# Groups of three, two and three gate units at fixed places, with W' parts, exponentials, h copies and w_in pairs moved

## The chip, the core and the metric

The kernel runs on one core of a Trainium2 chip. The metric is device time in microseconds (us), lower is better: the median of three runs. The engines are named as the profile names them: PE (TensorE matmuls), PEld (its weight loads), DVE (VectorE), ACT (ScalarE), POOL (GpSimd) and SP (SyncE, which issues transfers).

## What is computed

```python
def sm_attn(qq, kk, vv):                     # scale = 1/8
    s = scale * np.matmul(qq, kk.transpose(0, 1, 3, 2))
    s = s - np.max(s, axis=-1, keepdims=True)
    a = np.exp(s)
    a = a / (np.sum(a, axis=-1, keepdims=True) + 1e-09)
    return np.matmul(a, vv)
p_packed = sm_attn(p, k, v)                  # p: (8, 8, 32, 64); q, k, v: (8, 8, 576, 64)
out = sm_attn(q, p_packed, p_packed)
x = out.transpose(0, 2, 1, 3).reshape(4608, 512)
h = x @ w_in                                 # (512, 2048)
sp = np.maximum(h, 0.0) + np.log1p(np.exp(-np.abs(h)))
g = h * erf(sp)
result = g @ w_out                           # (2048, 512)
```

So an attention through 32 packed rows feeds a feed-forward layer whose gate is h times erf of softplus of h.

## The kernel before, in words

The second attention and `w_in` are merged: for each batch b and each quarter j of the 2048 columns, PE multiplies the packed values by `w_in` to W'(b, j), and h is W' times the second attention's weights. Each product is kept precise by splitting its operands in a high and a low half, so W' is copied out of PSUM twice: a high part (`wph`, line 594) and a low part (`wpl`, line 601), together "the W' parts".

The feed-forward work is cut into 128 units. A unit is 256 columns of h for half of a batch's tokens (288 columns), and from unit 32 on unit 32 + 16(b - 2) + 8c + i is the i-th of half c of batch b; h, t, hs, gh and gl of that unit are named b_c_i. The units run one after another. In step n:

- PE computes the two halves of h of unit n (12 matmuls, line 623) and then the output of unit n - 5 in four quarters d (24 matmuls, line 676);
- ACT copies the two halves of h out of PSUM into hs (line 633) and computes softplus (line 639);
- when n is in `ENDS`, a group of units is closed: ACT computes erf of every unit in it (line 642) and DVE multiplies it with h (the gate, line 646). One group means one load of ACT's softplus table and one of its erf table;
- DVE splits the gated value of unit n - 3 into gh (line 652) and gl (line 659).

h goes through two PSUM banks, so the first half of the h of unit n + 1 can start only when ACT has copied the first half of unit n. The output of a unit is copied with a scale (`put`: `ob`, lines 689 and 691) and sent off when its eighth unit is done.

The attention of a later batch is cut into pieces (`yield`), and tables of pairs (unit, place) say where each piece stands in the steps; so do tables for the W' products and their parts. Place 5 is behind the h copies, 0 and 1 behind the first output quarter, 3 behind the third, and 2 at the end of the step, behind the erfs and gates. One piece holds the two exponentials of the first attention (`a`, line 473, which need DVE's maximum `m`, line 448), and the next has PE's transposes of the result (`t`, line 423). The second attention has its exponential on line 317 (`ta`). An exponential needs another ACT table. From batch 4 on W' is multiplied from `w_in` in 16-bit pairs (`wi16`, lines 254 and 259), made by DVE in eight pieces. Instructions stand on each engine in the order in which the code is run.

Of the kernel before, what the change touches and what calls it, by code (L numbers as in the profile page):

```python
# [15 lines left out]
ALU = mybir.AluOpType  # L16
# [29 lines left out]
def tile_pack_attention_moe(ctx: ExitStack, tc: tile.TileContext, qT, kT, v, pT, w_in, w_out, outT):  # L46
    nc = tc.nc
    P = 128
    B, _, NC, S = qT.shape
    DFF = w_in.shape[1]  # L50
    DM = w_out.shape[1]
    HT = S // 2
# [13 lines left out]
    NB0 = 2  # L66
# [2 lines left out]
    ALONE = 2 * HB  # L69
    TAGS = ("hs", "hs", "hs", "t1", "t1", "t1", "hs", "hs")  # L70
    BANKS = {3: 0, 4: 2}
    ENDS = tuple(range(1, 16 * B, 3))
    BEGUN = 20

    cpool = ctx.enter_context(tc.tile_pool(name="const", bufs=1))
# [83 lines left out]
    rho, omega, gate_scales = {}, {}, {}  # L159
# [102 lines left out]
    def is_narrow(b, j):  # L262

        return b >= NB0 + 2
# [3 lines left out]
    def in_turn(ins):  # L268

        if functions:  # L270
# [9 lines left out]
    ATTEND = {  # L280
# [6 lines left out]
    SCORES = ((-12, 2), (-6, 0), (-6, 1), (-4, 0), (-4, 1))  # L287
    POOLED = ((-2, 3), (-2, 2), (-1, 3), (-1, 2), (0, 0), (0, 1))
    PACKED = ((1, 0), (1, 1), (2, 0), (2, 1), (4, 0), (4, 1))
    ATTEND_LATER = (  # L290
        SCORES + ((-4, 2), (-1, 5), (-1, 3), (-1, 2), (0, 0), (0, 1), (0, 3), (0, 2)) + PACKED
        + ((5, 2), (6, 2), (8, 5), (8, 3), (8, 2), (8, 2), (9, 2), (10, 2), (10, 2)),
        SCORES + ((-4, 2), (-2, 5)) + POOLED + PACKED
        + ((5, 2), (6, 2), (7, 5), (7, 2), (8, 2), (8, 2), (9, 2), (10, 2), (10, 2)),
        SCORES + ((-4, 2), (-3, 5)) + POOLED + PACKED
        + ((5, 2), (6, 2), (9, 5), (9, 3), (9, 2), (9, 2), (10, 2), (11, 2), (11, 2)))
    BESIDE = ((1, 1), (1, 3), (B - 1, 1), (B - 1, 3))
    JOINS = {2: (25, 27, 30, 32)}
    JOINS_LATER, PAIRED = (-6, -4, 2, 4), (-4, -4, 1, 1)
# [279 lines left out]
    def w_prime_parts(b, j):  # L579
        f0, n = PIECES[j]  # L580
        at = b, f0 // FB
        if at not in wp:
            wp[at] = [wpool.tile([P, 2, FB], F32R if b < NB0 else F16, name=f"wp{x}{b}_{j}", tag=f"wp{x}") for x in "hl"]
        parts = [w[:, :, f0 % FB:f0 % FB + n] for w in wp[at]]
        if len(raw[b, j]) == 3:
            return [parts + [raw[b, j][2][:, :, 0:n]]]
        return [[w[:, r, :] for w in parts] + [raw[b, j][r][:, 0:n]] for r in range(2)]

    def w_prime_high(b, j, copy=nc.scalar.copy):
        for hi, lo, ps in w_prime_parts(b, j):  # L590
            if b < NB0:
                copy(hi, ps)
            else:
                nc.vector.tensor_scalar(hi, ps, 2.0 ** -15 if is_narrow(b, j) else rho[b][:], None, op0=ALU.mult)  # L594

# [10 lines left out]
    def h_half(n, k):  # L606
        b, c, i = units[n][:3]
        if k == 0:
            turn = sum(n > e for e in ENDS) % 2
            tag = TAGS[n] if n < ALONE else "t1" if turn else "hs"  # L610
            rows[n] = tpool.tile([P, 2, HT], F32, name=f"hs{b}_{c}_{i}", tag=tag)
        f = (2 * i + k) * P
        j, fo = f // FB, f % FB
        whi, wlo = wp[b, j]
        if n in BANKS:
            ps = ps_o.tile([P, 512], F32, name=f"h{b}_{c}_{i}_{k}", tag=f"ps_o{BANKS[n] + k}")
        else:
            ps = ps_h.tile([P, 512], F32, name=f"h{b}_{c}_{i}_{k}", tag="ps_h")
        m = 0
        ahi, alo = a2[b]  # L620
        for r in range(2):
            for w, a in ((whi, ahi), (whi, alo), (wlo, ahi)):
                nc.tensor.matmul(ps[:, 0:HT], w[:, r, fo:fo + P], a[:, r, c * HT:(c + 1) * HT],  # L623
                                 start=(m == 0), stop=(m == 5))
                m += 1
        banks_of[n, k] = ps

    def h_copy(n, k, copy=nc.scalar.copy):
        dst, src = rows[n][:, k, :], banks_of.pop((n, k))[:, 0:HT]
        if n < GROUPED:  # L630
            copy(dst, src)  # L631
        else:
            nc.scalar.mul(dst, src, 2.0 ** -18)  # L633

    def softplus(n):
        b, c, i = units[n][:3]
        ts[n] = tpool.tile([P, 2, HT], F32, name=f"t{b}_{c}_{i}", tag="t0")
        scale = 1.0 if n < GROUPED else gate_scales[b][:, 0:1]
        in_turn(nc.scalar.activation(ts[n][:], rows[n][:], AF.Softplus, scale=scale))  # L639
# [22 lines left out]
    acc = {}  # L662
    begun = set()

    def o_part(n, d):

        b, c, i, first, last = units[n]
        g = gs[n]
        w_hi, w_lo = (wo_hi, wo_lo) if b < NB0 else (half_hi, half_lo)
        if first:  # L670
            acc[b, c, d] = ps_o.tile([P, 512], F32, name=f"o{b}_{c}_{i}_{d}", tag=f"ps_o{d}")
        for k in range(2):
            f = 2 * i + k
            terms = [(wo, g[0])] if len(g) == 1 else [(w_hi, g[0]), (w_hi, g[1]), (w_lo, g[0])]
            for m, (w, gg) in enumerate(terms):
                nc.tensor.matmul(acc[b, c, d][:, 0:HT], w[f][:, d * P:(d + 1) * P], gg[:, k, :],  # L676
                                 start=(first and k == 0 and m == 0),
                                 stop=(last and k == 1 and m == len(terms) - 1))

    def put(n, d, fast=False):  # L680

        b, c, i = units[n][:3]
        t0 = b * S + c * HT
        ob = tpool.tile([P, HT], F32, name=f"ob{b}_{c}_{i}_{d}", tag="ob", bufs=NDM)
        if b < NB0:
            nc.scalar.copy(ob[:], acc[b, c, d][:, 0:HT])  # L686
        else:
            if fast:
                nc.vector.tensor_scalar(ob[:], acc[b, c, d][:, 0:HT], omega[b][:], None, op0=ALU.mult)
            else:  # L690
                nc.scalar.mul(ob[:], acc[b, c, d][:, 0:HT], omega[b][:])
        where = outT[d * P:(d + 1) * P, t0:t0 + HT]
        if (b, c, d) in begun:
            nc.gpsimd.dma_start(where, ob[:], accum_op=ALU.add)
        else:
            (nc.gpsimd if b < NB0 else nc.sync).dma_start(where, ob[:])
        begun.add((b, c, d))


    group = []  # L700

    def split(n):
        split_high(n)
        split_low(n)

    def step(n, m):

        if n < len(units):
            for k in range(2):
                h_half(n, k)  # L710
                h_copy(n, k)
            do(n, 5)
            group.append(n)
        for d in range(NDM):
            o_part(m, d)
            if units[m][4]:
                put(m, d, n in ENDS)
            if d == 0:
                do(n, 0)
                do(n, 1)  # L720
                if n < len(units):
                    softplus(n)
            elif d == 2:
                do(n, 3)
        if m + 2 < len(units):
            split(m + 2)
        if n in ENDS:
            for part in (erf, gate):
                for x in group:
                    part(x)  # L730
            group.clear()
        do(n, 2)
# [19 lines left out]
    def slot(n, where):  # L752
        return plan.setdefault((n, where), [])

    for b in range(NB0, B):
        for j in range(NFB):
            n = JOINS[b][j] if b in JOINS else first_use[b] + (JOINS_LATER if b < B - 1 else PAIRED)[j]
            behind = 1 if (b, j) in BESIDE else 2
            for where, part in ((0, w_prime), (behind, w_prime_high), (behind, w_prime_low)):
                slot(n, where).append((part, b, j))  # L760
    for b in range(NB0, B):
        base = first_use[b - 1]
        for n, where in ATTEND.get(b) or [(base + n, where) for n, where in ATTEND_LATER[base % 3]]:
            slot(n, where).append((attend, b))

    for n, k in ((21, 5), (21, 6), (22, 7)):
# [14 lines left out]
        slot(high, 0 if i < 6 else 5).append((halve_high, i))  # L781
        slot(low, 1).append((halve_low, i))
    slot(28, 2).append((in_weights,))
    for m, n in enumerate((39, 41, 42, 44, 45, 47, 48, 50)):
        slot(n, 1).append((narrow_high, m % 4, m // 4))
        slot(n, 1).append((narrow_low, m % 4, m // 4))
    for b in range(NB0 + 1, B):
# [3 lines left out]
    def do(n, where):  # L791
        for part, *args in plan.pop((n, where), []):
            part(*args)
# [44 lines left out]
    for n in range(BEGUN, len(units) + LAG):  # L838
        step(n, n - LAG)
# [39 lines left out]
```

## Time and profile before

| | before |
|---|---|
| median of three runs | 696.69 us (696.46 to 698.27) |
| the profiled execution | 696.33 us, its span 694.5 us |
| PE busy | 674.4 us, 97% of the span |
| DVE busy | 517.1 us, 74% |
| ACT busy | 493.3 us, 71% |
| POOL busy | 53.0 us, 8% |

The span runs from the first to the last instruction of the profiled execution; 1.8 us of its time lie around it. Shares of busy time are means over a beginning (attention of two batches, weights being loaded and split) and the long run of units behind it, from about 200 us on.

### The profile page before, as it was taken

What the parts mean: (1) busy time and instruction counts of PE and PEld (TensorE: products, weight loads), DVE (VectorE), ACT (ScalarE), POOL (GpSimd) and SP (SyncE); (2) the same over time, 40 slices, a digit from 0 to 9 for tenths busy, and PEclk for the clock granted to TensorE, in tenths of its full rate; (3) what the DMA queues carried; (4) which work ended last, traced back from release to release, by engine and by line L of the source; (5) the groups of instructions that cost most, each with busy time, mean ns of one, the idle gap of its engine ahead of it and who ended that gap; (6) DMA issues with size and microseconds to landing.
All of it is one profiled execution on the core that took longest, in us unless ns stands there. A gap on an engine that the chain in (4) does not pass through costs nothing.

```text
span 694.5 us, 15657 instructions
## 1 busy us (share of the span) xinstructions
PE 674.4 (97%) x6570; PEld 537.2 (77%) x6570; DVE 517.1 (74%) x822; ACT 493.3 (71%) x814; POOL 53.0 (8%) x78
## 2 busy tenths in 40 slices
PE   8899999999999999999999999899999999999998
PEld 6587989998889776777777777667777777777776
DVE  5999998989996799786765688556684768564343
ACT  2899878966577687656685775756877667767671
POOL 2031123110442000000000000000000000000000
PEclk9999999999999999999999999999999999999999
DMA  9996556376333502230022302113021100001010
GB/s 328 399 331 213 160 179 214 106 255 179 51 63 64 138 2 94 87 98 2 19 77 86 100 1 90 43 45 99 2 90 53 35 1 10 27 1 35 1 35 35
DMA packets 34310, 66.81 MB, mean 96 GB/s; under 512 B 4032, under 2 KB 13248, under 8 KB 34240
## 3 DMA queue, kind: packets, MB, share of 16 engines
q1 hardware_dynamic: 29600, 56.31, 24.2%
q0 software_dynamic: 4352, 8.92, 4.9%
q8 instruction: 51, 0.84, 0.5%
q10 hardware_dynamic: 288, 0.59, 0.2%
q14 instruction: 19, 0.16, 0.1%
HBM read 49.81 MB, written 15.99 MB: 95 GB/s over the span
## 4 chain that ended last, share of the span: by engine, by line
PE 69%; DVE 16%; ACT 4%; DMA 4%; issue 4%; POOL 1%; SPq 0%; POOLq 0%; DVEq 0%; ACTq 0%
PE o L676 43%; PE h L623 20%; DVE hs L646 3%; PE wp L575 3%; DVE gl L659 2%; DMA wi<-w_in 2%; DMA k<-kT 2%; DVE wpl L601 1%; DVE wph L594 1%; PE p L435 1%; PE s L533 1%; DVE gh L652 1%; ACT t L642 1%; DMA scratch<-wo 1%; DVE wi L259 1%
## 5 line engine op out<-in xcount | busy, mean ns | idle before, releaser
L676 PE MATMUL o<-gh,woh 128*128 128x288 f16 x1536 | 303.3, 286 | 0.8 <-DVE gh L652 0.8
L676 PEld LDWEIGHTS <-woh 128*128 128x128 f16 x2304 | 223.6, 98 | 65.9 <-issue 10.4
L676 PE MATMUL o<-gl,woh 128*128 128x288 f16 x768 | 219.6, 286 | 0.5 <-DVE gl L659 0.5
L623 PE MATMUL h<-a2h,wph 128*128 128x288 f16 (+1 forms) x512 | 149.1, 291 | 3.1 <-ACT hs L633 1.1
L623 PE MATMUL h<-a2h,wpl 128*128 128x288 f16 (+1 forms) x512 | 147.8, 289 | 3.3 <-DVE wpl L601 2.6
L633 ACT ACTIVATE hs<-h 128x288 f32<-128x288 f32 x192 | 73.7, 405 | 106.5 <-PE h L623 106.3
L623 PE MATMUL h<-a2l,wph 128*128 128x288 f16 (+1 forms) x512 | 147.5, 288 | 0.0
L652 DVE CAST gh<-hs 128x576 f16<-128x576 f32 (+1 forms) x117 | 53.3, 455 | 113.9 <-PE o L676 113.5
L659 DVE TENSOR_TENSOR gl<-hs,gh 128x576 f16<-128x576 f32 (+1 forms) x124 | 98.1, 791 | 4.4 <-ACT gh L652 0.5
L676 PE MATMUL o<-gh,wohl 128*128 128x288 f32 x448 | 99.2, 300 | 0.9 <-ACT ob L686 0.8
L623 PEld LDWEIGHTS <-wph 128*128 128x128 f16 x768 | 74.4, 98 | 22.2 <-DVE wph L594 2.1
L646 DVE TENSOR_TENSOR hs<-t,hs 128x576 f32<-128x576 f32 x128 | 90.0, 750 | 0.7 <-ACT t L642 0.7
L676 PEld LDWEIGHTS o<-gh,wohl 128*128 128x128 f32 x448 | 74.5, 188 | 7.7 <-issue 2.7
L642 ACT ACTIVATE t<-t 128x576 f32<-128x576 f32 x128 | 78.9, 674 | 0.5
L639 ACT ACTIVATE t<-hs,gs 128x576 f32<-128x576 f32 x96 | 74.5, 776 | 2.0
L676 PE MATMUL o<-gl,wohl 128*128 128x288 f32 x224 | 66.2, 295 | 0.1
L639 ACT ACT_TABLE_LOAD x45 | 57.7, 1283 | 3.0 <-DVE hs L646 2.1
L642 ACT ACT_TABLE_LOAD x44 | 56.5, 1283 | 0.8
L623 PEld LDWEIGHTS <-wpl 128*128 128x128 f16 x384 | 37.6, 98 | 12.9 <-DVE wpl L601 3.5
L676 PEld LDWEIGHTS o<-gl,wohl 128*128 128x128 f32 x224 | 42.2, 188 | 0.3 <-DVE gl L659 0.3
L631 ACT COPY hs<-h 128x288 f32<-128x288 f32 x45 | 17.0, 397 | 15.4 <-PE h L623 15.1
L623 PEld LDWEIGHTS h<-a2h,wph 128*128 128x128 f32 x128 | 24.0, 188 | 3.9 <-issue 1.3
(129 smaller groups left out, 734.3 us busy)
## 6 DMA issues: line engine op xcount, KB each, us to landing
q<-qT SPq DMA_DIRECT2D x32, 288.0 KB, 4.3
k<-kT SPq DMA_DIRECT2D x30, 288.0 KB, 4.7
wos<-w_out SPq DMA_DIRECT2D x16, 512.0 KB, 6.2
outT<-ob SPq DMA_DIRECT2D x48, 144.0 KB, 2.2
v<-v SPq DMA_DIRECT2D x24, 256.0 KB, 4.6
wi<-w_in SPq DMA_DIRECT2D x12, 512.0 KB, 6.6
outT<-ob POOLq DMA_DIRECT2D x32, 144.0 KB, 4.0
scratch<-wo POOLq DMA_DIRECT2D x16, 256.0 KB, 3.9
```

The source lines that it names most:

```text
L259: nc.vector.scalar_tensor_tensor(narrow[c, k][:, 1], w_in_sb[:, c, 2 * k * FB:2 * (k + 1) * FB], sigma_in[:], narrow[c, k][:, 0], op0=ALU. ...
L435: nc.tensor.matmul(po[NK * c:NK * c + NK, 64 * r:64 * r + 64], a1t[0:n, r, j, NK * c:NK * c + NK], values[j][0:n, 64 * (2 * c + r):64 * (2 ...
L575: nc.tensor.matmul(ps[r][NK * c:NK * c + NK, 0:n], p[:, NK * c:NK * c + NK], w, start=(m == 0), stop=(m == len(terms) - 1), skip_group_che ...
L623: nc.tensor.matmul(ps[:, 0:HT], w[:, r, fo:fo + P], a[:, r, c * HT:(c + 1) * HT], start=(m == 0), stop=(m == 5))
L631: copy(dst, src)
L633: nc.scalar.mul(dst, src, 2.0 ** -18)
L639: in_turn(nc.scalar.activation(ts[n][:], rows[n][:], AF.Softplus, scale=scale))
L642: in_turn(nc.scalar.activation(ts[n][:], ts[n][:], AF.Erf))
L646: nc.vector.tensor_tensor(hs[:], ts.pop(n)[:], hs[:], op=ALU.mult)
L652: copy(ghi[:], gs[n][0][:])
L659: nc.vector.tensor_tensor(glo[:], hs[:], ghi[:], op=ALU.subtract)
L676: nc.tensor.matmul(acc[b, c, d][:, 0:HT], w[f][:, d * P:(d + 1) * P], gg[:, k, :], start=(first and k == 0 and m == 0), stop=(last and k = ...
```

## The change

Groups: up to unit 31 they end as before; then 33, and from 34 on every unit whose number leaves 0, 3 or 5 when divided by 8, so groups hold 3, 2 and 3 units. The outputs that DVE scaled in steps at a group's end are scaled by ACT. The high part of batch 2's W' is made by ACT. The parts of the later W' stand at place 3 (ahead of a step's erfs and gates) instead of place 2. One table places the later attentions: their exponentials stand at the end of steps that close a group. For two units in 16 the h copies are handed DVE's copy function, in place of ACT's. The eight pieces of `w_in`'s pairs stand in units 46, 47, 49, 50 and 62 to 65.

```diff
-    ENDS = tuple(range(1, 16 * B, 3))
+    ENDS = tuple(range(1, 32, 3)) + (33,) + tuple(n for n in range(34, 16 * B) if n % 8 in (0, 3, 5)) + (16 * B - 1,)
...
-    ATTEND_LATER = (
-        SCORES + ((-4, 2), (-1, 5), (-1, 3), (-1, 2), (0, 0), (0, 1), (0, 3), (0, 2)) + PACKED
...
+    ATTEND_LATER = ((-12, 2), (-6, 0), (-6, 1), (-4, 0), (-4, 1), (-4, 2), (-3, 2), (-1, 0), (-1, 1), (-1, 3), (-1, 2),
+                    (0, 0), (0, 1), (1, 0), (1, 1), (2, 0), (2, 1), (4, 0), (4, 1),
+                    (5, 2), (6, 2), (8, 2), (9, 3), (9, 2), (9, 2), (10, 2), (11, 2), (11, 2))
...
+            elif b == NB0:
+                nc.scalar.mul(hi, ps, rho[b][:])
...
+        elif copy is nc.vector.tensor_copy:
+            nc.vector.tensor_scalar(dst, src, 2.0 ** -18, None, op0=ALU.mult)
         else:
             nc.scalar.mul(dst, src, 2.0 ** -18)
...
-            if fast:
-                nc.vector.tensor_scalar(ob[:], acc[b, c, d][:, 0:HT], omega[b][:], None, op0=ALU.mult)
-            else:
-                nc.scalar.mul(ob[:], acc[b, c, d][:, 0:HT], omega[b][:])
+            nc.scalar.mul(ob[:], acc[b, c, d][:, 0:HT], omega[b][:])
...
+    AFTER = [b + n for b in range(2 * 16, 16 * B, 16) for n in (9, 14)]
...
-                h_copy(n, k)
+                h_copy(n, k, nc.vector.tensor_copy if n in AFTER else nc.scalar.copy)
...
-            behind = 1 if (b, j) in BESIDE else 2
+            behind = 1 if (b, j) in BESIDE else 2 if b == NB0 else 3
...
-    for m, n in enumerate((39, 41, 42, 44, 45, 47, 48, 50)):
+    for m, n in enumerate((46, 47, 49, 50, 62, 63, 64, 65)):
```

Three places of the order show the moves. The first is on ACT, in units 93 and 94 (5_1_5 and 5_1_6, ahead of batch 6), with the exponentials `a1_7` of the first attention of batch 7. Before, from the softplus of unit 94 on:

```order
L639 ACTIVATE t5_1_6_6937<-hs5_1_6_6914,gs5_5550 128x576
L642 ACT_TABLE_LOAD
L642 ACTIVATE t5_1_4_6811<-t5_1_4_6811 128x576
L642 ACTIVATE t5_1_5_6887<-t5_1_5_6887 128x576
L642 ACTIVATE t5_1_6_6937<-t5_1_6_6937 128x576
L633 ACTIVATE hs5_1_7_6967<-h5_1_7_0_6968 128x288
L633 ACTIVATE hs5_1_7_6967<-h5_1_7_1_6976 128x288
L473 ACT_TABLE_LOAD
L473 ACTIVATE a1_7_6643,sm7_6859<-a1_7_6643,m7_6858 128x576 x2
L639 ACT_TABLE_LOAD
```

In the changed kernel, from the softplus of unit 93 on:

```order
L636 ACTIVATE t5_1_5_6887<-hs5_1_5_6863,gs5_5547 128x576
L639 ACT_TABLE_LOAD
L639 ACTIVATE t5_1_4_6811<-t5_1_4_6811 128x576
L639 ACTIVATE t5_1_5_6887<-t5_1_5_6887 128x576
L466 ACT_TABLE_LOAD
L466 ACTIVATE a1_7_6643,sm7_6859<-a1_7_6643,m7_6858 128x576 x2
L630 ACTIVATE hs5_1_6_6920<-h5_1_6_0_6921 128x288
L630 ACTIVATE hs5_1_6_6920<-h5_1_6_1_6929 128x288
L636 ACT_TABLE_LOAD
L636 ACTIVATE t5_1_6_6943<-hs5_1_6_6920,gs5_5547 128x576
```

The exponentials have moved from behind the copies of unit 95 to ahead of the copies of unit 94. Unit 94 is one of those in `AFTER`, and its two copies stand on ACT.

The second is on DVE, at the third quarter of batch 5's W', which the h of unit 84 needs. Before, behind the split of unit 78:

```order
L540 STREAM_TRANSPOSE ta6_6129<-s2_0_6_0_6130 128x288
L540 STREAM_TRANSPOSE ta6_6129<-s2_0_6_1_6131 128x288
L652 CAST gh4_1_7_6162<-hs4_1_7_5860 128x576
L659 TENSOR_TENSOR gl4_1_7_6164<-hs4_1_7_5860,gh4_1_7_6162 128x576
L646 TENSOR_TENSOR hs5_0_0_5919<-t5_0_0_5997,hs5_0_0_5919 128x576
L646 TENSOR_TENSOR hs5_0_1_6021<-t5_0_1_6057,hs5_0_1_6021 128x576
L646 TENSOR_TENSOR hs5_0_2_6081<-t5_0_2_6142,hs5_0_2_6081 128x576
L594 TENSOR_SCALAR wph5_2_6172<-wp5_2_6104 128x1024
L601 SCALAR_TENSOR_TENSOR wpl5_2_6173<-wp5_2_6104,wph5_2_6172 128x1024
```

In the changed kernel:

```order
L533 STREAM_TRANSPOSE ta6_6131<-s2_0_6_0_6132 128x288
L533 STREAM_TRANSPOSE ta6_6131<-s2_0_6_1_6133 128x288
L589 TENSOR_SCALAR wph5_2_6158<-wp5_2_6106 128x1024
L596 SCALAR_TENSOR_TENSOR wpl5_2_6159<-wp5_2_6106,wph5_2_6158 128x1024
L649 CAST gh4_1_7_6168<-hs4_1_7_5854 128x576
L656 TENSOR_TENSOR gl4_1_7_6170<-hs4_1_7_5854,gh4_1_7_6168 128x576
```

The two parts now stand ahead of the split and of the gates.

The third is on DVE, in units 43 and 44, where h of batch 2 is split while batch 3 is prepared. Before:

```order
L594 TENSOR_SCALAR wph3_1_3525<-wp3_1_3468,rho3_3349 128x1024
L601 SCALAR_TENSOR_TENSOR wpl3_1_3526<-wp3_1_3468,rho3_3349,wph3_1_3525 128x1024
L448 TENSOR_REDUCE m4_3539<-a1_4_3333 128x2
L449 TENSOR_SCALAR m4_3539<-m4_3539 128x2
L254 TENSOR_SCALAR wi16_0_1_3568<-w_in_sb_82,sigma_in_93 128x1024
L259 SCALAR_TENSOR_TENSOR wi16_0_1_3568<-w_in_sb_82,sigma_in_93,wi16_0_1_3568 128x1024
L652 CAST gh2_1_2_3594<-hs2_1_2_3301 128x576
L659 TENSOR_TENSOR gl2_1_2_3596<-hs2_1_2_3301,gh2_1_2_3594 128x576
```

In the changed kernel:

```order
L589 TENSOR_SCALAR wph3_1_3500<-wp3_1_3459,rho3_3341 128x1024
L596 SCALAR_TENSOR_TENSOR wpl3_1_3501<-wp3_1_3459,rho3_3341,wph3_1_3500 128x1024
L649 CAST gh2_1_1_3513<-hs2_1_1_3245 128x576
L656 TENSOR_TENSOR gl2_1_1_3515<-hs2_1_1_3245,gh2_1_1_3513 128x576
L441 TENSOR_REDUCE m4_3527<-a1_4_3328 128x2
L442 TENSOR_SCALAR m4_3527<-m4_3527 128x2
L649 CAST gh2_1_2_3579<-hs2_1_2_3296 128x576
L656 TENSOR_TENSOR gl2_1_2_3581<-hs2_1_2_3296,gh2_1_2_3579 128x576
```

No piece of `w_in`'s pairs stands ahead of the split of unit 42 (2_1_2) now, and the split of unit 41 has moved behind the W' parts.

Over the whole program ACT has 113 table loads in place of 103 and still all 192 copies of h from unit 32 on; DVE has no scaling of `ob` left.

## Rows read from the trace of the kernel before

**Rows 1.** Busy time (instructions) by engine in two 20 us stretches.

```profile
core 0: us, PE busy (x) PEld busy (x) DVE busy (x) ACT busy (x) POOL busy (x), PEclk, DMA share, GB/s
...
420.00:440.00 20.00, 18.25 (x176) 13.50 (x174) 15.64 (x23) 12.06 (x22) 0.00 (x0) 1.00 0.25 79
640.00:660.00 20.00, 20.00 (x166) 15.98 (x164) 8.06 (x13) 11.79 (x20) 0.00 (x0) 1.00 0.00 1
```

**Rows 2.** PE's waits from 222 us on: total us, times, longest.

```profile
PE h L623 <- DVE wpl L601: 2.6, 3, 0.9
PE t L423 <- ACT a L473: 2.3, 6, 0.6
PE h L623 <- ACT hs L633: 1.1, 1, 1.1
PE h L623 <- DVE wph L594: 1.1, 2, 0.6
PE o L676 <- DVE gh L652: 0.8, 1, 0.8
PE o L676 <- DVE gl L659: 0.5, 1, 0.5
PE p L511 <- DVE norm L507: 0.4, 2, 0.2
```

**Rows 3.** PE's waits from 160 to 222 us.

```profile
PE row_out L192 <- DVE top_out L185: 1.2, 1, 1.2
```

**Rows 4.** Timeline of PE, units 94 and 95: start us, us, [wait and releaser].

```profile
514.45 0.29 PE L623 MATMUL h<-a2h,wph 128*128 128x288 f16 x1
...
518.86 0.29 PE L623 MATMUL h<-a2h,wph 128*128 128x288 f16 x1
...
523.31 0.55 PE L423 MATMUL t<-ident,a 128*128 128x128 f32 x3 [0.61 <-ACT a L473]
```

**Rows 5.** Timeline of DVE and PE, units 82 to 84.

```profile
458.47 0.85 DVE L540 STREAM_TRANSPOSE ta<-s 128x288 f32<-128x288 f32 x2 [2.31 <-PE s L533]
...
465.10 1.22 DVE L601 SCALAR_TENSOR_TENSOR wpl<-wp,wph 128x1024 f16<-128x1024 f32 x1
465.13 0.30 PE L623 MATMUL h<-a2h,wph 128*128 128x288 f16 x1
```

**Rows 6.** Timeline of ACT, unit 77.

```profile
435.39 0.78 ACT L473 ACTIVATE a<-a,m 128x576 f32<-128x576 f32 x1 [3.29 <-DVE m L449]
```

**Rows 7.** Timeline of DVE, unit 45.

```profile
274.17 1.28 DVE L259 SCALAR_TENSOR_TENSOR wi<-w_in_sb,sigma_in,wi 128x1024 f16<-128x1024 f32 x1
```

**Rows 8.** Timeline of DVE, unit 26.

```profile
165.31 1.28 DVE L594 TENSOR_SCALAR wph<-wp,rho 128x1024 f16<-128x1024 f32 x1
```

**Rows 9.** Timeline of ACT, units 93 to 95.

```profile
512.70 0.78 ACT L639 ACTIVATE t<-hs,gs 128x576 f32<-128x576 f32 x1
515.38 0.41 ACT L633 ACTIVATE hs<-h 128x288 f32<-128x288 f32 x1 [1.91 <-PE h L623]
...
517.35 1.28 ACT L642 ACT_TABLE_LOAD   x1
518.65 1.83 ACT L642 ACTIVATE t<-t 128x576 f32<-128x576 f32 x3
...
521.09 1.28 ACT L473 ACT_TABLE_LOAD   x1
522.39 0.77 ACT L473 ACTIVATE a<-a,m 128x576 f32<-128x576 f32 x1
...
524.03 1.28 ACT L639 ACT_TABLE_LOAD   x1
```

**Rows 10.** ACT's groups from 222 us on: busy us, mean ns | idle before.

```profile
L642 ACT ACT_TABLE_LOAD x31 | 39.8, 1283 | 0.5
...
L691 ACT ACTIVATE ob<-o,omega 128x288 f32<-128x288 f32 x32 | 15.0, 497 | 16.7 <-PE o L676 16.7
...
L317 ACT ACTIVATE ta<-ta 128x1152 f32<-128x1152 f32 x5 | 5.8, 1164 | 1.3 <-DVE ta L315 1.2
```

**Rows 11.** Busy time by engine from 222 us on, columns as in rows 1.

```profile
222.00:694.50 472.50, 460.26 (x4520) 352.19 (x4519) 319.81 (x503) 321.81 (x521) 2.90 (x4) 1.00 0.16 50
```

More of the change, by code (lines that the diff above doesn't have):

```diff
@@ L283, in tile_pack_attention_moe @@
             (29, 1), (29, 2)),
[1 row of a table removed]
[1 row of a table added]
             (36, 0), (36, 1), (37, 0), (37, 1), (38, 0), (38, 0), (38, 0), (38, 1),
[1 row of a table removed]
-    SCORES = ((-12, 2), (-6, 0), (-6, 1), (-4, 0), (-4, 1))
-    POOLED = ((-2, 3), (-2, 2), (-1, 3), (-1, 2), (0, 0), (0, 1))
-    PACKED = ((1, 0), (1, 1), (2, 0), (2, 1), (4, 0), (4, 1))
-    ATTEND_LATER = (
-        SCORES + ((-4, 2), (-1, 5), (-1, 3), (-1, 2), (0, 0), (0, 1), (0, 3), (0, 2)) + PACKED
[L292 to L296, printed above, removed]
[1 row of a table added]
+    ATTEND_LATER = ((-12, 2), (-6, 0), (-6, 1), (-4, 0), (-4, 1), (-4, 2), (-3, 2), (-1, 0), (-1, 1), (-1, 3), (-1, 2),
+                    (0, 0), (0, 1), (1, 0), (1, 1), (2, 0), (2, 1), (4, 0), (4, 1),
+                    (5, 2), (6, 2), (8, 2), (9, 3), (9, 2), (9, 2), (10, 2), (11, 2), (11, 2))
     BESIDE = ((1, 1), (1, 3), (B - 1, 1), (B - 1, 3))
@@ L678, in o_part, with put @@
                                  stop=(last and k == 1 and m == len(terms) - 1))
-    def put(n, d, fast=False):
+    def put(n, d):
         b, c, i = units[n][:3]
@@ L716, in step @@
             if units[m][4]:
-                put(m, d, n in ENDS)
+                put(m, d)
             if d == 0:
@@ L762, in tile_pack_attention_moe @@
         base = first_use[b - 1]
-        for n, where in ATTEND.get(b) or [(base + n, where) for n, where in ATTEND_LATER[base % 3]]:
+        for n, where in ATTEND.get(b) or [(base + n, where) for n, where in ATTEND_LATER]:
             slot(n, where).append((attend, b))
```

4 rows, old and new, of the table ATTEND are left out of this document.

## The prediction

> **What bounds the kernel now.** I read four views in this order. The first is busy time in 20 us stretches. Where no attention runs, PE is busy for all of its 20.00 us, its granted clock is 1.00, that is 2.4 GHz, and 165 to 166 matmuls fit, one each 0.12 us; at 420 us it is busy for 18.25 us at the same clock [rows 1]. So PE sets the pace everywhere, DVE and ACT have spare time (319.8 and 321.8 of 472.5 us busy from 222 us on, 68% each [rows 11]), and nothing can be won but what PE waits.
>
> The second view, PE's own waits, says how much that is. From 222 us on there are 16 waits, 8.8 us together [rows 2]. A wait costs more than its row: a matmul's row lasts 0.29 us [rows 4], while in a full stream the next one starts after 0.12 us, so a stop loses the wait and about 0.16 us of overlap. 8.8 + 16 x 0.16 = 11.4 us is all that the stretch holds. Ahead of it one more wait matters, 1.2 us, in which PE waits for DVE's tallest weight, `top_out` [rows 3].
>
> The third view, the timelines, says why PE waits. There are three causes. (a) The W' parts stand behind three gates on DVE: `wpl` runs from 465.10, and the h that needs it has already begun at 465.13 [rows 5]. That is 2.6 + 1.1 us in five waits. (b) The exponentials of the first attention stand directly ahead of PE's transposes: PE waits 0.61 us at 523.31 [rows 4], in six waits 2.3 us [rows 2]. Once it is worse: ACT itself waits 3.29 us for DVE's maximum with the copies of h queued behind the exponential [rows 6], and the 1.1 us wait of h for hs is that. (c) DVE is late in the forties because pieces of `w_in`'s pairs stand ahead of the splits [rows 7]: 0.8 + 0.5 us. Two small waits for `norm`, 0.4 us, come from the one of the three old tables that places the normalisation behind a unit's last outputs.
>
> **The change, part by part.** *W' parts.* In unit 82 the transposes `ta` start on DVE at 458.47 and take 0.85 us [rows 5]. The two parts, 1.22 us each, now follow at once, so they end near 461.8; the h of unit 84 starts at 465.13. They have 3.3 us to spare, and what they push back, one split and the gates, is needed more than a unit later, at 4.41 us a unit (518.86 - 514.45 [rows 4]). Batches 3 and 6 are the same with the last quarter. Gain: 3.7 + 5 x 0.16 = 4.5 us.
>
> *Exponentials two units earlier.* They now end two units ahead of the transposes instead of directly ahead, so PE's six waits go: 2.3 + 6 x 0.16 = 3.3 us. The maximum `m` now never stands behind a group's gates, since unit base - 4 closes no group, so the 3.29 us stop on ACT goes and with it 1.1 + 0.16 = 1.3 us. But the exponentials now stand ahead of copies of h, and this I work out from the units where before has everything but the move. Softplus of unit 93 starts at 512.70 [rows 9]. Then come: softplus 0.78, a table load 1.30 (517.35 to 518.65), two erfs 1.22 (two thirds of 1.83), a table load 1.30, two exponentials 1.64 (522.39 to 524.03), the first copy of unit 94 0.41. That ends at 519.35. The h of unit 95 would start at 518.86 [rows 4]. So PE waits 0.5 us, in each of four batches: a cost of 2.0 us. Behind the next softplus ACT is on time again: it has no more than a copy, a load and a softplus to do in that unit.
>
> *The copies on DVE don't take place.* The order shows the copies of unit 94 on ACT. `copy is nc.vector.tensor_copy` compares two method objects that are made anew at each access, which is never true, so the branch for DVE is dead. Were it alive, those 2.0 us would be hidden; I count them in full.
>
> *The other exponential,* `ta`, now stands behind a group's three erfs and ahead of copies. With unit 94's times: the erfs end at 518.65 + 1.83 = 520.48; load 1.30, exponential 1.16 [rows 10], copy 0.41 end at 523.35, 8.90 us behind the unit's start at 514.45, where two units are 8.82. That is late by 0.1 us, five times: 0.4 us (nothing to 0.8).
>
> *More groups.* 113 loads in place of 103 are 10 x 1.283 = 12.8 us on ACT, and 16 outputs moved from DVE are 16 x 0.497 = 8.0 us [rows 10]. ACT goes from 321.8 to 342.6 us in a stretch of some 462: 74%. Outside the two chains above this lies beside PE: a group of two has one load pair for two units, (2 x 1.28 + 2 x (0.82 + 0.78 + 0.61)) / 2 = 3.5 us a unit against PE's 4.41. If that cover were gone, 20.8 us would be the price.
>
> *The Trainium skill on table loads.* In these rows a load delays what follows by 1.30 us and nothing else: 517.35 to 518.65, 521.09 to 522.39 [rows 9]. The Trainium skill, ScalarE: Activation LUTs, section "What ACT_TABLE_LOAD costs", gives 1283 ns and adds a drain of 1380 ns, 2.66 us for each change of set, and asks to batch calls by set, which speaks against more and smaller groups. By that figure the ten loads would cost 26.6 us on ACT. The trace agrees with the 1283 ns and shows no drain, so the sum goes by the rows.
>
> *Pairs of w_in, and `norm`.* The pairs leave units 39 to 45, where they made DVE late, and the one table that is left normalises early: 0.8 + 0.5 + 0.4 + 4 x 0.16 = 2.3 us gained. Where the pairs go, units 46 to 50 and 62 to 65, DVE takes at least 1.28 us more a unit. The tightest place that I find is unit 50: from the scores on, DVE has `ta` 0.85, a pair (1.28 [rows 7], and an estimated 0.7 for its first half) and two parts of 1.28 [rows 8], 5.4 us, before the h of unit 52. PE has three output quarters (18 matmuls of 0.12, 2.2 us) and a unit of 4.41, 6.6 us. So about 1 us is spare, and I cost it at nothing; if DVE comes 2 us later than I think, it is 1 us there and as much at the splits.
>
> *High part of batch 2 on ACT.* In unit 26 it stood 1.28 us on DVE ahead of `top_out` [rows 8], in a stretch in which DVE never rests, so `top_out` comes 1.28 us earlier and the 1.2 us wait goes nearly whole: 1.2 + 0.1 = 1.3 us. ACT takes it while it waits for PE; bounds nothing to 1.4.
>
> *The sum.* 4.5 + 3.3 + 1.3 + 2.3 + 1.3 = 12.7 us gained, 2.0 + 0.4 = 2.4 us paid: 10.3 us. From the profiled execution's 696.33 that gives 686.0; the median of the runs is 0.36 above it, so 686.4 us.
>
> **The rivals.** *ACT keeps its waits (16%).* The extra loads leave ACT as late as it is now at the first attention, and all that it costs PE now, 3.4 + 7 x 0.16 = 4.5 us, stays beside the new 2.4: 690.9. For it speaks that ACT's chains have only tenths of a us to spare; against it, that the transposes have two whole units now. *DVE is late at the new places of the pairs (9%).* 1 us at the W' parts and as much at the splits in either place, 4 x (1.0 - 0.3), since part of it would hide the 0.5 us behind it: 686.4 + 2.8 = 689.2. For it, 1 us of spare time is little; against it, DVE rests for 32% of the stretch. *Slower (5%): ACT falls behind at both exponentials.* If ACT reaches the erf groups x us later than worked out, the loss is 4 x (0.5 + x) for the first and 5 x (0.1 + x) for the second exponential; at x = 1.1 this is the whole 12.7, and at x = 2 the time is 704. It would need copies that come late because ACT still has outputs of the unit before; in unit 92 the trace has exactly this, and softplus of unit 93 is at 512.70 with it, which is why I don't believe in more. By the page on ScalarE named above, two loads in each chain would make x 2.8 and the time 712; the rows show none of it, so I give it one of these five in a hundred. *Nothing comes of it (3%).* Every removed wait is followed by another as long: 696.7.
>
> **How the numbers follow.** The forecast has 67%: 686.4, itself between 683.6 (12.7 gained and nothing paid, 684.0, less 0.4 by which eleven rounded rows may be short) and 688.7 (half of the W' gain missing). With the two rivals on the same side it reaches to 690.9; what is left out is slower, nothing, and a gain beyond PE's waits. So 683.6 to 691.0. A measurement of this kernel can't tell less than about 0.3% (2.1 us) from no change. Faster by more than that: 67 + 16 + 9 = 92%; the same 3%; slower 5%.
>
> **What would show it.** PE's waits after: none for `wph`, `wpl`, `gh`, `gl`, none of `t` for the exponentials, `row_out` under 0.2 us, and four new waits of h for hs of about 0.5 us at the first halves of units 47, 63, 79 and 95. On ACT, 192 copies from h with a scale, 10 more loads, no wait for `m`. DVE should still rest, mostly for PE's outputs. The prediction is wrong if the waits of h for hs add to more than 5 us, if PE waits for W' parts near units 50 to 54, or if table loads take longer than 1.3 us to the next instruction.

## The result and the profile after

The changed kernel takes 686.01 us (median of four runs, 685.83 to 686.26) where before takes 696.7: a ratio of 0.984, 95% interval 0.983 to 0.986. The forecast was 686.4 us in a range of 683.6 to 691.0. The profiled execution has a span of 684.1 us, 10.4 less than before. One execution of all those below, of the kernel with the W' parts alone, ran at a granted clock of 0.557 and took 1141.82 us; it is left out of that kernel's ratio.

First the busy time of each engine in two stretches of the changed kernel, from 222 us to its end and the 20 us that stand in [rows 1] (columns as there), then all of PE's waits from 222 us on.

```profile
222.00:684.10 462.10, 456.14 (x4507) 351.09 (x4505) 310.15 (x483) 338.20 (x543) 2.60 (x3) 1.00 0.16 50
420.00:440.00 20.00, 19.70 (x232) 15.88 (x229) 11.49 (x18) 18.02 (x31) 0.00 (x0) 1.00 0.22 73
```

```profile
PE h L618 <- DVE wpl L596: 1.3, 1, 1.3
PE h L618 <- ACT hs L630: 1.2, 4, 0.3
```

Sixteen waits of 8.8 us [rows 2] have become five of 2.5 us: 8.8 - 2.5 + 11 x 0.16 = 8.1 us of the 10.4. ACT's busy time has risen from 321.8 us in 472.5 [rows 11] to 338.2 in 462.1; of the waits listed it costs PE only the second row.

Ahead of 222 us `row_out` no longer waits (1.2 us before [rows 3]), and the wait for `ob` is shorter. The first line is from before, the other two are all of PE's waits from 160 to 222 us in the changed kernel:

```profile
PE o L676 <- ACT ob L686: 0.8, 1, 0.8
PE h L618 <- ACT hs L626: 0.5, 1, 0.5
PE o L673 <- ACT ob L683: 0.2, 1, 0.2
```

Waits can be checked against the starts of h, that is, the time at which PE begins the first matmul of a unit. Here is unit 34, before and after:

```profile
207.70 0.30 PE L623 MATMUL h<-a2h,wph 128*128 128x288 f16 x1
205.88 0.30 PE L618 MATMUL h<-a2h,wph 128*128 128x288 f16 x1
```

Unit 26 still starts at the same time in both (161.83 and 161.85), so 1.8 us of the gain lie between units 26 and 34, 1.3 of them at `row_out` and 0.5 at `ob`. The other 8.7 us lie behind. The view of waits gives 8.1 of them; it doesn't list every stop: a matmul's row lasts 0.29 us and the next one follows after 0.12, so a stop shows only as far as it exceeds about 0.16 us, and a gap of 0.1 us between rows is not listed.

The 0.3 us waits are the ones that the prediction worked out behind the exponentials. These are the timeline of ACT in units 93 and 94 and, last, of PE at the h of unit 95:

```profile
503.65 0.78 ACT L636 ACTIVATE t<-hs,gs 128x576 f32<-128x576 f32 x1
504.44 1.28 ACT L639 ACT_TABLE_LOAD   x1
505.74 1.26 ACT L639 ACTIVATE t<-t 128x576 f32<-128x576 f32 x2
507.01 1.28 ACT L466 ACT_TABLE_LOAD   x1
508.31 0.77 ACT L466 ACTIVATE a<-a,m 128x576 f32<-128x576 f32 x1
...
509.84 0.68 ACT L630 ACTIVATE hs<-h 128x288 f32<-128x288 f32 x2
...
510.28 0.28 PE L618 MATMUL h<-a2h,wph 128*128 128x288 f16 x1 [0.30 <-ACT hs L630]
```

Softplus to first copy takes 509.84 - 503.65 = 6.19 us, where the sum from [rows 9] gave 6.24. PE loses 0.30 + 0.16 = 0.46 us, worked out as 0.5.

The other wait, 1.3 us, the prediction did not have. The timeline of DVE and, last, of PE, units 108 and 109:

```profile
574.42 2.09 DVE L643 TENSOR_TENSOR hs<-t,hs 128x576 f32<-128x576 f32 x3
...
576.42 0.75 DVE L328 CAST a2h<-tb 128x1152 f16<-128x1152 f32 x1
577.21 1.36 DVE L330 TENSOR_TENSOR a2l<-tb,a2h 128x1152 f16<-128x1152 f32 x1
...
578.49 1.28 DVE L589 TENSOR_SCALAR wph<-wp 128x512 f16<-128x512 f32 x2
...
579.68 1.28 DVE L596 SCALAR_TENSOR_TENSOR wpl<-wp,wph 128x512 f16<-128x512 f32 x2
580.42 0.30 PE L618 MATMUL h<-a2h,wph 128*128 128x288 f16 x1 [1.28 <-DVE wpl L596]
```

Of the later batches' products W', only two quarters of batch 7, the second being one, are put in the two PSUM banks that h uses (`BESIDE`). Their parts free the banks, and those of the second quarter now stand behind three gates and the last two pieces of batch 7's attention, which the new table puts at the end of unit 107, a unit that closes a group.

### The profile page after: what moved, and what is told of

It is laid out like the page before. It is cut to its first block, busy times and chain, and to the rows that moved or that the text cites. A ratio compares the mean times of both kernels' runs of the same rounds, so it can differ in the third digit from the quotient of the medians.

```text
span 684.1 us, 15658 instructions
## 1 busy us (share of the span) xinstructions
PE 672.0 (98%) x6570; PEld 538.4 (79%) x6570; DVE 504.2 (74%) x802; ACT 516.7 (76%) x844; POOL 53.7 (8%) x78
## 4 chain that ended last, share of the span: by engine, by line
PE 77%; ACT 9%; DVE 8%; issue 3%; DMA 2%; POOL 1%; POOLq 0%; ACTq 0%; DVEq 0%
PE o L673 47%; PE h L618 22%; PE wp L568 3%; DVE hs L643 2%; PE p L428 1%; PE s L526 1%; ACT t L636 1%; ACT a L466 1%; ACT t L639 1%; ACT L466 1%; ACT L639 1%; DMA v<-v 1%; DVE gh L649 1%; DMA q<-qT 1%; ACT L636 1%
## 5 line engine op out<-in xcount | busy, mean ns | idle before, releaser
L649 DVE CAST gh<-hs 128x576 f16<-128x576 f32 (+1 forms) x117 | 55.8, 477 | 125.9 <-PE o L673 125.6
L656 DVE TENSOR_TENSOR gl<-hs,gh 128x576 f16<-128x576 f32 (+1 forms) x124 | 96.3, 776 | 4.4 <-ACT gh L649 0.5
L636 ACT ACT_TABLE_LOAD x50 | 64.2, 1283 | 1.2 <-DVE hs L643 0.3
L639 ACT ACT_TABLE_LOAD x49 | 62.9, 1283 | 0.9
L685 ACT ACTIVATE ob<-o,omega 128x288 f32<-128x288 f32 x48 | 22.2, 494 | 15.7 <-PE o L673 15.5
```

Source lines behind the costliest of these rows:

```text
L639: in_turn(nc.scalar.activation(ts[n][:], ts[n][:], AF.Erf))
L649: copy(ghi[:], gs[n][0][:])
L656: nc.vector.tensor_tensor(glo[:], hs[:], ghi[:], op=ALU.subtract)
```

## The experiments

Each was timed in five rounds. Ratios are to the kernel before in the same rounds; the ratio of the changed kernel is 0.984.

**The dead branch made alive.**

```diff
-    def h_copy(n, k, copy=nc.scalar.copy):
+    def h_copy(n, k, copy=nc.scalar.copy, on_dve=False):
...
-        elif copy is nc.vector.tensor_copy:
+        elif on_dve:
...
-                h_copy(n, k, nc.vector.tensor_copy if n in AFTER else nc.scalar.copy)
+                h_copy(n, k, on_dve=n in AFTER)
```

> The changed kernel with DVE's branch for the h copies made reachable, so that the 24 copies of the units in AFTER really run on DVE. If the four waits of h for hs (0.30 us each, with 0.16 of overlap 1.9 us together) come from ACT's copies standing behind the exponentials: 684.1, and no wait of h for hs at units 47, 63, 79 and 95. Rival: DVE, which takes its queue in order, waits for PE's h itself and holds up the splits behind the copies: 686.0 or more.

Measured: 684.14 us, ratio 0.981 (0.980 to 0.983). Of PE's waits from 222 us on the one for `wpl` is left; the four for hs are gone. The expected 684.1 was met, so the copies behind the exponentials are the cause, and the part of the change that did nothing was worth 1.9 us. The starts of h give 2.2 us from unit 34 on: 1.9 at units 47, 63, 79 and 95, and about 0.4 around units 42, 58, 74, 90 and 106, whose h starts 0.04 us late in the changed kernel, behind copies that follow the other exponential, `ta`. The two copies on DVE, in unit 94:

```profile
507.25 0.81 DVE L628 TENSOR_SCALAR hs<-h 128x288 f32<-128x288 f32 x2
```

**The exponentials behind the copies.**

```diff
-    ATTEND_LATER = (... (-4, 2), (-3, 2), (-1, 0), ...
+    ATTEND_LATER = (... (-4, 2), (-2, 5), (-1, 0), ...
```

> The changed kernel with the first attention's exponentials one place later, behind the h copies of the next unit and ahead of its softplus; the number of table loads stays 113. By the same cause: 684.1, the four waits gone, and PE's transposes still without a wait, since by the rows of before the exponentials end about 1.6 us ahead of them. Rival: ACT has too much to do around the exponentials wherever they stand, the waits move to the unit behind: 686.0.

Measured: 684.68 us, ratio 0.982 (0.981 to 0.983). The four waits are gone here too and no other has come. That is 1.3 us less than the changed kernel, not the 1.9 of the four waits. But its profiled execution comes to the wait for `ob` at 204.1 us, where the changed kernel's comes to it at 203.4, in a part of the program that is the same. The starts of h settle the size: unit 46 starts 0.75 us later than in the changed kernel and unit 127 1.10 us earlier, so the move gives the 1.9 us that were expected.

**Batch 7's last pieces one unit later.**

```diff
-        ... [(base + n, where) for n, where in ATTEND_LATER]:
+        ... [(base + n, where) for n, where in (
+                ATTEND_LATER if b < B - 1 else ATTEND_LATER[:-2] + ((12, 2), (12, 2)))]:
```

> The changed kernel with the last two pieces of batch 7's second attention (a2h, a2l) one unit later, so that they no longer stand ahead of the W' parts whose PSUM banks the h of unit 109 needs. If those 2.1 us on DVE are what PE waits for at 580 us: 1.28 + 0.16 = 1.4 us less, 684.6. Rival: the three gates ahead of them are enough to make DVE late: 685.5, and the wait is still 0.5 us or more.

Measured: 684.95 us, ratio 0.983 (0.982 to 0.985). The wait for `wpl` is gone and nothing took its place. The medians give 1.1 us; by the starts of h it is 1.45 (unit 108 starts 0.43 us later than in the changed kernel, unit 110 1.02 us earlier). So the gates alone do not make PE wait. The three gates take DVE 2.09 us and the two pieces 2.1, and no run moved the gates in their stead: that the pieces alone would be enough is not shown.

**Both.** The last two edits together.

> The changed kernel with both edits, exponentials behind the copies and batch 7's pieces one unit later. If the two causes are apart: 686.0 - 1.9 - 1.4 = 682.7, and from 222 us on PE has no wait of more than 0.1 us left. If one of the waits only moves: 684.1 to 684.6.

Measured: 683.27 us (683.01 to 683.74), ratio 0.980 (0.979 to 0.982), expected 682.7. These are all of PE's waits from 160 us to the end; both lie ahead of 222 us:

```profile
PE h L618 <- ACT hs L626: 0.5, 1, 0.5
PE o L673 <- ACT ob L683: 0.2, 1, 0.2
```

Between units 46 and 127 it gains 3.3 us on the changed kernel by the starts of h, the sum of both. It is the fastest kernel of this study, and from 222 us on the view of waits names nothing more to win; what is left there is PE's own work and stops too short for a row, such as 0.04 us at the h of five units.

**The W' parts alone, in the kernel before.**

```diff
-            behind = 1 if (b, j) in BESIDE else 2
+            behind = 1 if (b, j) in BESIDE else 2 if b == NB0 else 3
```

> The kernel before with one part of the change alone: the W' parts of batches 3 to 6 at place 3, ahead of erfs and gates. If their place behind three gates is what PE waited for: five waits gone, 3.7 + 5 x 0.16 = 4.5 us, 692.2. Rival: the gates go first on DVE only a little later, and the split and the gates now come late instead: 694 to 697, with waits for gh or gl.

Measured: 692.68 us, ratio 0.993 (0.992 to 0.995), 4.5 us less than before's 697.22 in the same rounds. Its only trace is of the execution at a granted clock of 0.557, so no row shows which waits went. The time is the one expected, so in the kernel before the place ahead of the gates is enough by itself.

**The W' parts back, in the changed kernel.** The opposite edit of that line.

> The changed kernel with the W' parts back at place 2, the end of the step; groups and all else as changed. If the place of the parts gives the gain: PE's waits for wph and wpl come back, 4.5 us, 690.5. Rival: since units +2 and +4 of a batch close no group any more, place 2 stands behind one split (1.2 us) and no gates: nothing comes back, 686.0.

Measured: 686.08 us, ratio 0.985 (0.983 to 0.987): nothing came back. From 222 us on PE's waits are those of the changed kernel to the tenth, and the starts of h agree within 0.1 us from unit 10 on.

So the prediction's reason holds for the kernel before and not for the changed one: there the groups' ends have already taken the gates from ahead of the parts.

**The groups alone, in the kernel before.** The line of `ENDS` as in the change.

> The kernel before with the groups' ends of the changed kernel alone; the attention stays where it was, so that ACT loads 119 tables. W' parts stay at place 2. If their place is what counts and not the groups: PE's five waits for wph and wpl stay, and with the exponentials now within groups 697 to 700. Rival: units +2 and +4 of a batch close no group now, so the gates no longer stand ahead of the parts: the five waits go without any move of the parts, 692.2, or up to 696 where the exponentials come out worse.

Measured: 703.44 us, ratio 1.009 (1.008 to 1.011). PE's waits from 222 us on:

```profile
PE h L623 <- ACT hs L633: 6.0, 3, 3.7
PE p L509 <- DVE a L500: 3.5, 2, 1.8
PE t L423 <- ACT a L473: 2.4, 6, 0.7
PE o L676 <- DVE gh L652: 0.8, 1, 0.8
PE o L676 <- DVE gl L659: 0.5, 1, 0.5
PE p L511 <- DVE norm L507: 0.4, 2, 0.2
```

No wait for `wph` or `wpl` is left, which the rival said and my theory did not. But the old places of the attention's pieces no longer fit: waits of h for ACT grow from 1.1 to 6.0 us, and DVE's normalisation `a` is late by 3.5. The groups alone lose; in the changed kernel they stand with the attention's new table, and no run has the new table without them.

**The pairs alone, in the kernel before.**

```diff
-    for m, n in enumerate((39, 41, 42, 44, 45, 47, 48, 50)):
+    for m, n in enumerate((46, 47, 49, 50, 62, 63, 64, 65)):
```

> The kernel before with the w_in pairs alone at units 46, 47, 49, 50 and 62 to 65. If the pairs ahead of the splits made DVE late at 275 us: the waits for gh and gl go, 0.8 + 0.5 + 2 x 0.16 = 1.6 us, 695.1. Rival: DVE is late at the new places, above all at the W' parts of batch 3: 696.7 or more.

Measured: 697.61 us, ratio 1.001 (1.000 to 1.002): no gain. PE's waits from 222 us on:

```profile
PE h L623 <- DVE wpl L601: 3.2, 4, 0.9
PE t L423 <- ACT a L473: 3.1, 8, 0.6
PE h L623 <- ACT hs L633: 1.1, 1, 1.1
PE h L623 <- DVE wph L594: 1.1, 2, 0.6
PE p L511 <- DVE norm L507: 0.4, 2, 0.2
```

Against [rows 2], `gh` and `gl` are gone (1.3 us), but `wpl` has one more wait (0.6) and `t` two (0.8). The waits for `gh` and `gl` stood in unit 47 (0.78 and 0.51 us). PE, no longer held there, comes to the transposes of the same unit before ACT has their exponentials, for which before had no wait in this unit. The new wait for `wpl` is behind pieces of the pairs in units 49 and 50:

```profile
280.75 0.55 PE L423 MATMUL t<-ident,a 128*128 128x128 f32 x3 [0.61 <-ACT a L473]
305.36 0.30 PE L623 MATMUL h<-a2h,wpl 128*128 128x288 f16 x1 [0.62 <-DVE wpl L601]
```

**The pairs back, in the changed kernel.** The opposite edit.

> The changed kernel with the w_in pairs back at units 39, 41, 42, 44, 45, 47, 48 and 50, all else as changed. If their place gives a gain in the changed kernel, DVE is late again near 270 us and PE's waits for gh and gl return: 1.3 + 2 x 0.16 = 1.6 us, 687.6. Rival, after the pairs alone gave nothing in the kernel before: with gates of batch 2's last units and the W' parts in other places, DVE has room there and another wait or none stands in their stead: 685.8 to 686.3.

Measured: 688.06 us, ratio 0.988 (0.986 to 0.989), 2 us more than the changed kernel. Two waits are back beside those that it has, and those for hs add up to 1.4 us in place of 1.2:

```profile
PE o L673 <- DVE gh L649: 0.5, 1, 0.5
PE o L673 <- DVE gl L656: 0.5, 1, 0.5
```

By the starts of h the loss is 1.5 us at units 46 and 47, as expected, and 0.3 us come back at unit 66. There, in the changed kernel, PE stops within the product W' for the last piece of the pairs, which DVE ends at 370.12; the stop is too short for a row of waits. The changed kernel first, then this run:

```profile
369.67 1.12 PE L568 MATMUL wp<-wi,pt 64*32 64x512 f16 x24
371.41 0.84 PE L568 MATMUL wp<-wi,pt 64*32 64x512 f16 x24
```

So the move of the pairs gives its gain in the changed kernel and not in the kernel before. That the moved exponentials and W' parts make the difference follows from the two waits shown above; no run tests either of them together with the pairs alone.

**High part of batch 2 on ACT alone, in the kernel before.**

```diff
             if b < NB0:
                 copy(hi, ps)
+            elif b == NB0:
+                nc.scalar.mul(hi, ps, rho[b][:])
```

> The kernel before with the high part of batch 2's W' alone on ACT. If DVE's chain ahead of top_out is what PE waits for at 174 us: the wait of 1.2 us goes, 695.4. Rival: ACT, which now makes 1.1 us more in units 25 and 27, is late with exponential or copies instead: 696.7.

Measured: 695.37 us, ratio 0.997 (0.996 to 0.998), 1.9 us less than before in the same rounds. The wait of `row_out` is gone from 160 to 222 us, and the one for `ob`, 0.75 us at 205 us in the kernel before, is 0.47. I had counted the first alone. By the starts of h the two are 1.3 and 0.3 us, 1.6 in all.

**The exponentials two units later, in the changed kernel.**

```diff
-    ATTEND_LATER = (... (-4, 2), (-3, 2), (-1, 0), ...
+    ATTEND_LATER = (... (-4, 2), (-1, 5), (-1, 0), ...
```

> The changed kernel with the first attention's exponentials two units later, in the unit of the transposes, where one of the old tables had them. If the two units between exponentials and transposes give the gain: PE waits about 2.9 us for the exponentials in each of four batches, less the 0.47 us of the h copies, 695.5. Rival: the gain came from the maximum that is now made early, and the distance matters little: 686 to 688.

Measured: 696.39 us, ratio 0.9986 (0.998 to 1.000): 10.4 us more than the changed kernel, nearly all that the change gains. PE's waits from 222 us on, and the timeline of ACT and PE in unit 95:

```profile
PE t L416 <- ACT a L466: 8.4, 7, 1.9
PE h L618 <- DVE wpl L596: 1.3, 1, 1.3
```

```profile
519.87 0.41 ACT L630 ACTIVATE hs<-h 128x288 f32<-128x288 f32 x1 [0.32 <-PE h L618]
520.30 1.28 ACT L466 ACT_TABLE_LOAD   x1
521.60 0.77 ACT L466 ACTIVATE a<-a,m 128x576 f32<-128x576 f32 x1
...
522.52 0.55 PE L416 MATMUL t<-ident,a 128*128 128x128 f32 x3 [1.95 <-ACT a L466]
```

By the starts of h the move costs 2.1 us in each of four batches, 8.5 in all. Another 1.4 us come in unit 47 of the profiled execution alone: behind its wait of 1.95 us the granted clock is 0.50 for 3.4 us (shown in the last section). Most of this kernel's executions have 0.998 over their span, as this one has, so the median probably holds such a stretch too. The maximum `m` is early in this kernel as well, so the distance between exponentials and transposes counts, and not `m` alone.

**A group for each unit from 113 on.**

```diff
-    ... if n % 8 in (0, 3, 5)) + (16 * B - 1,)
+    ... if n % 8 in (0, 3, 5) or n >= 113) + (16 * B - 1,)
```

> The changed kernel with a group for every single unit from 113 on: 18 more table loads (131), no attention there. By the rows a load holds ACT for 1.30 us, so ACT takes 0.72 + 0.70 + 1.30 + 0.61 + 1.30 = 4.6 us a unit where PE takes 4.41: up to 0.25 us in 15 units, 686 to 690. If each change of set cost 2.66 us, as the Trainium skill (ScalarE: Activation LUTs, What ACT_TABLE_LOAD costs) has it, ACT would take 7.4 us a unit: 45 us more, 731.

Measured: 693.91 us, ratio 0.995 (0.994 to 0.997). The timeline of ACT for one unit and the load that opens the next:

```profile
646.98 1.28 ACT L639 ACT_TABLE_LOAD   x1
648.27 0.68 ACT L639 ACTIVATE t<-t 128x576 f32<-128x576 f32 x1
648.86 0.69 ACT L630 ACTIVATE hs<-h 128x288 f32<-128x288 f32 x2
649.57 1.28 ACT L636 ACT_TABLE_LOAD   x1
650.87 0.78 ACT L636 ACTIVATE t<-hs,gs 128x576 f32<-128x576 f32 x1
651.66 1.28 ACT L639 ACT_TABLE_LOAD   x1
```

A load delays what follows by 1.29 and 1.30 us, as in [rows 9]. A unit takes ACT 651.66 - 646.98 = 4.68 us, where PE needs 4.41. The cost is 7.9 us, more than the 4 that I allowed. By the starts of h, ten units from 116 on start 0.28 us late each, 2.8 us, which is what 4.68 against 4.41 gives; these stops are too short for a row of waits. I left out the four outputs that ACT also copies in each of units 116 and 124 (PE waits 1.6 us for `ob` and 1.4 for hs behind them, 3.7 with the overlap lost) and the end of the kernel (a wait of 0.5 for `gl`, 0.6 with it). That is 7.1 us; the rest of this execution's difference, 1.7 us, is there at unit 10 already. The cost is far from the 45 us that 2.66 us a load would have cost. The measurement decides against the drain that the Trainium skill (ScalarE: Activation LUTs, What ACT_TABLE_LOAD costs) adds, and for the 1283 ns that it gives for the load.

## Why the prediction was right, and where it was not

**That PE's waits are all there is to gain** was right: 8.1 of 10.4 us are listed waits that went from 222 us on, and 1.8 lie at the two waits ahead of it.

**W' parts, 4.5 us.** The waits went and the size is measured (4.5 us alone; 4.8 by the starts of h around units 54, 84 and 102 in the changed kernel), but the step named an edit that the changed kernel doesn't need. Either the parts' place or the groups' ends is enough; with both, the place is worth nothing.

**Exponentials two units earlier, 3.3 + 1.3 - 2.0 us.** All seven waits went, four of 0.30 us came, at the four units named. The 3.3 was 0.3 too small, since the second stop among a unit's transposes costs more than its row and 0.16: from the first start to the matmul behind them, the six of unit 62 take 1.14 us before and those of unit 63 in the changed kernel 0.66, so that stop loses 0.48 where its row has 0.21. Put two units later, the exponentials cost 8.5 us.

**The dead branch, 2.0 us counted in full.** Made alive it gives 1.9.

**The other exponential, 0.4 us.** The view of waits has nothing in units 42, 58, 74, 90 and 106, but the starts have. The h of unit 74 follows the matmul ahead of it after 0.16 us instead of 0.12, and the same 0.04 us is lost in the other four:

```profile
405.53 0.29 PE L673 MATMUL o<-gh,woh 128*128 128x288 f16 x1
405.69 0.28 PE L618 MATMUL h<-a2h,wph 128*128 128x288 f16 x1
```

That is 0.2 us at the five h alone; with the copies on DVE the five stops are gone and 0.4 us are gained around them. The term was right to some tenths.

**More groups, nothing.** Right: of 16.4 us more of ACT in the stretch PE sees only the stops behind the two exponentials, which have terms of their own.

**Pairs and norm, 2.3 us.** In the changed kernel the waits went, and 2 us come back when the pairs do. In the kernel before the same move gives nothing; I argued it as if it stood alone. The place that I called the tightest, unit 50, costs nothing; unit 66, which I did not name, costs 0.3 us. For `norm`, whose two waits went, there is no run by itself.

**High part on ACT, 1.3 us.** Right for `row_out` (1.3 us by the starts of h). I left out the wait for `ob`, which it shortens by 0.3 us; in the changed kernel that wait is 0.5 us shorter.

**What the sum left out** is the wait of 1.28 + 0.16 us at unit 109. I followed the W' parts that moved and not the pieces that the new table put ahead of those that did not. It and the last pair at unit 66 made the kernel 1.7 us slower than the sum. About as much went the other way, by the starts as well: 0.5 for `ob`, 0.3 for the transposes, 0.3 for the W' parts, 0.2 for the four new waits, which are a little shorter than worked out, and 0.4 at unit 38, where no wait is listed. The mechanism of each term held, but that the forecast of 686.4 is right to 0.4 us is in part luck.

## What to carry to other kernels

Where one engine is full, add up its waits, give each the overlap that a stop loses, and then check for each edit whether another edit already takes the same wait away: two of this change's parts did the same, and one gave nothing without the others. Follow what a new table puts ahead of instructions that did not move, above all ahead of those that free a PSUM bank. And read the order for what was really built: a function compared by `is` to a method made anew at each access never matches.

## What was not expected of the hardware

The beginning differs by more between executions than many edits are worth. The kernel with the pairs alone has the same program as before up to unit 39, yet its profiled execution came to the wait for `ob` at 208.0 us where before's came to it at 205.2. Of these 2.8 us 1.4 are there at unit 10. The others come around 178 us, where the granted clock is 0.50 (1.2 GHz) for 3.4 us. Two more traces have one such stretch in the midst of the units. Here are the pairs alone, the exponentials two units later, and the groups alone (columns as in [rows 1]):

```profile
177.65:181.00 3.35, 3.35 (x15) 3.35 (x15) 3.28 (x5) 0.79 (x3) 0.00 (x0) 0.50 0.02 5
276.40:279.75 3.35, 3.34 (x15) 2.12 (x14) 0.00 (x0) 2.34 (x4) 0.00 (x0) 0.50 0.00 0
293.95:297.30 3.35, 3.35 (x17) 2.12 (x15) 1.66 (x6) 1.53 (x2) 0.00 (x0) 0.50 0.00 0
```

In the second a matmul of 288 columns starts every 0.24 us in the stretch and every 0.12 around it. Ahead of the three stretches PE had waited 1.24, 1.95 and 1.75 us within the last two microseconds. But before's profiled execution waits 1.23 us at the same place as the first and keeps a granted clock of 1.00, so what brings the stretch on is not shown. In a mean clock of 0.997 or 0.998 over the span it is easily missed. The starts of one unit in two traces, and medians over rounds, tell such edits apart; two spans do not.
